# A linear-attention and channel-mix kernel: the arithmetic of the start moved between engines, and a new written order

## The chip, the cores and the metric

The kernel runs on one core of a Trainium2 chip. The metric is the device time of one execution in microseconds (us). A core has five engines that run side by side and meet through semaphores: TensorE (PE; its weight loads are PEld), VectorE (DVE), ScalarE (ACT), GpSimd (POOL) and SyncE (SP). Transfers between device memory (HBM) and on-chip memory (SBUF) are issued by SP, ACT or POOL and moved by 16 transfer engines (DMA).

## The reference

The input is q, k, v of shape (8 batches, 8 heads, 576 positions, 64), then the weights of a channel mix. The attention part is linear: a softmax of q over the head dimension, a softmax of k over the positions, and two small products. The channel mix shifts the sequence by one position, mixes it with two vectors mu, and runs three products.

```python
q_s = exp(q - max(q, -1));  q_s /= sum(q_s, -1)
k_s = exp(k - max(k, 2));   k_s /= sum(k_s, 2)
kv  = einsum('bhsd,bhse->bhde', k_s, v)
x   = einsum('bhsd,bhde->bhse', q_s, kv)        # as (B, S, 512)
x_prev = x shifted by one position
xk = mu_k * x + (1 - mu_k) * x_prev
xr = mu_r * x + (1 - mu_r) * x_prev
k  = maximum(xk @ w_k, 0)                       # 512 -> 1024
v  = k * k @ w_v                                # 1024 -> 512
r  = sigmoid(xr @ w_r)                          # 512 -> 512
out = r * v                                     # float32
```

The kernel leaves out the subtraction of the maxima, which cancels, and writes the sigmoid as a tanh.

## The kernel before, in words

The work of a batch b is split into two halves of its heads, g = 0 and 1, and in batches 0 and 1 each load and exponential is split once more (n = 0, 1). The names in the written order are built from these digits: `expq001` is the exponential of q for batch 0, half 0, part 1. For one (b, g):

- `load…q/k/v`: the transfers into a ring of eleven raw buffers `raw_a` to `raw_k` (L201), and `load0gv` into `vb` (L216). Batches 1 to 7 are loaded through GpSimd's queue, batch 0's q and k through the queues of SyncE and ScalarE. Eight semaphores serve GpSimd's transfers in turn, so a transfer is not issued before the one eight places earlier has landed.
- `expq`, `expk` (ScalarE, L325), `cast` (ScalarE, L331: v to bf16), `rsum`, `rrec`, `scale` (VectorE, L340, L344, L349: the softmax of q).
- `T`, `KV`, `Z` (TensorE): transpose of q, k times v, and the sums of k; for later batches one block `TKV` or `B`. `rz` and `kvn` or `w` (VectorE) normalise, `qt` (ScalarE) copies the transpose out.
- In batches 0 and 1 the mixing with mu is folded into the small weights: `wp…0` for xk and `wp…1` for xr (L466, two instructions each) multiply the normalised kv by mu and by 1 - mu; `X…0`, `X…1` (L478) are the products, and `x…` copies them into `xk` and `xr`, the first part on ScalarE and the second on VectorE (L488, L491). These need `wide` (a matmul that spreads mu over all partitions), `widecopy` (ScalarE, L279) and `rest` (L275: 1 - mu).
- Later batches use `xb`, `xs`, `edge`, `diff`, `sc`, `mix` instead, with mu as a column (`muload`, `mu`, `mucopy`).

The channel mix runs over units of up to 512 positions. In unit i, `ki0` to `ki7` (TensorE, L600) are the eight column blocks of x @ w_k, each four matmuls; in units 0 and 1 the first four are cut into two halves (`k01`, `k01.2`), the first needing only g = 0. `relu` (ScalarE, L587) and `sq` (VectorE, L591) follow. `r` (L632) and `v` (L652) are the other products, `th` (ScalarE, L637) the tanh, `o` (VectorE, L658) the gated output, `st` the store. The weights come through GpSimd's queue too: `wk00` to `wk11` (tiles `wk_aa`, `wk_ab`, `wk_ba`, `wk_bb`), `wr`, and `wv0` to `wv2` (`wv_a` to `wv_c`).

Nothing is scheduled at run time. `ORDER` is a string of some 950 names that fixes the order on every engine and in every queue; the digits behind a colon are the buffer that the step takes (`k01:2` takes PSUM bank 2, `mm_c`), `ACT!load…` puts a load in ScalarE's queue, and `fill.4^expq001` makes a step wait for another. An engine works through its names strictly in this order, so a step that waits for a transfer holds all that stands behind it on its engine. `fill` (L291) is a matmul of zeros that nobody reads; before the change seventeen of them stand among the first steps, held by steps of the softmax.

## Time and profile before

| | |
|---|---|
| time, median of 3 | 200.34 us (200.0 to 200.4) |
| the profiled execution's own time | 199.95 us |
| its span, first to last instruction | 198.2 us |
| TensorE busy | 186.0 us, 94% of the span |
| VectorE, ScalarE, GpSimd busy | 150.7, 146.3, 45.8 us |
| moved by the transfer engines | 40.13 MB, mean 202 GB/s |

A row of the order in time gives the start in us, the duration in us, the engine, the line of the kernel, the operation, its output and inputs with their shapes, and in brackets how long the engine was idle before it and what ended that. Rows of several like instructions are merged (x8). A row of the busy time by stage gives the stage, its length, then the busy time of each engine with the number of instructions, the granted TensorE clock, the busy share of the transfer engines (above 1 where packets of several queues overlap), and the GB/s that they moved. Buffer letters are part of the names (`mm_a` is PSUM bank 0, `raw_k` the eleventh raw buffer).

### The profile page before, as it was taken

The numbers are of one execution on the slowest core, as the hardware profiler recorded it, in microseconds if no ns is written. First come the engines' busy times: TensorE is split into PE (matmuls) and PEld (weight loads), VectorE is DVE, ScalarE is ACT, GpSimd is POOL, SyncE is SP. The second block draws the span as 40 slices with busy tenths as digits, with TensorE's granted clock in tenths as the row PEclk, the third lists the DMA queues.
The fourth block names the chain that finished last, engine by engine and source line by source line (L and its number), as shares of the span: only waits on it lengthen the run. The fifth ranks groups of instructions, "written<-read, shape, count | busy, mean of one in ns | idle before, by whom it ended". The sixth has DMA issues, their size and how long they took to land.

```text
span 198.2 us, 5164 instructions
## 1 busy us (share of the span) xinstructions
PE 186.0 (94%) x2060; PEld 93.2 (47%) x2084; DVE 150.7 (76%) x342; ACT 146.3 (74%) x225; POOL 45.8 (23%) x75
## 2 busy tenths in 40 slices
PE   1898999999999999999999999999999999999992
PEld 0374445434544544445565545554444544444751
DVE  0797468999989999999999995999825459732531
ACT  2678898799999999999999497877624762662340
POOL 7449357954324302712000000000000000000000
PEclk9999999999999999999999999999999999999999
DMA  6999999999999997899932230422044013402513
GB/s 200 310 289 288 273 341 202 393 394 398 416 390 390 401 412 281 291 392 406 369 98 55 59 77 3 106 56 53 3 108 108 0 29 80 106 2 56 122 37 106
DMA packets 16544, 40.13 MB, mean 202 GB/s; under 512 B 2300, under 2 KB 5640, under 8 KB 16520
## 3 DMA queue, kind: packets, MB, share of 16 engines
q0 software_dynamic: 9440, 27.99, 42.5%
q1 hardware_dynamic: 6120, 10.07, 18.5%
q10 hardware_dynamic: 960, 1.74, 2.6%
q8 instruction: 16, 0.26, 0.5%
q14 instruction: 8, 0.07, 0.1%
HBM read 33.56 MB, written 9.44 MB: 217 GB/s over the span
## 4 chain that ended last, share of the span: by engine, by line
PE 51%; issue 1%; ACT 0%; DVE 0%
PE mm_b L652 7%; PE mm_a L652 6%; PE mm_a L600 5%; PE mm_b L600 4%; PE mm_d L652 4%; PE mm_c L600 4%; PE mm_d L600 4%; PE mm_c L632 3%; PE mm_c L652 3%; PE mm_d L632 3%; PE mm_a L632 2%; PE mm_b L632 1%; PE att_b L516 1%; PE att_a L516 1%; PE att_a L390 1%
## 5 line engine op out<-in xcount | busy, mean ns | idle before, releaser
L652 PEld LDWEIGHTS <-k_a 128*128 128x128 bf16 x144 | 13.7, 98 | 16.9 <-DVE k_a L591 0.6
L632 PEld LDWEIGHTS <-xr 128*128 128x128 bf16 x144 | 13.9, 98 | 16.4 <-issue 0.2
L652 PEld LDWEIGHTS <-k_b 128*128 128x128 bf16 x152 | 14.3, 98 | 15.1 <-issue 0.6
L632 PE MATMUL mm_c<-wr,xr 128*128 128x512 bf16 x48 | 13.0, 379 | 0.2
L600 PEld LDWEIGHTS <-wk_bb 128*128 128x128 bf16 x80 | 7.8, 98 | 7.7
L600 PEld LDWEIGHTS <-wk_ab 128*128 128x128 bf16 x80 | 7.7, 98 | 8.1 <-DVE xk L488 0.6
L600 PEld LDWEIGHTS <-wk_ba 128*128 128x128 bf16 x80 | 7.7, 98 | 7.8 <-issue 0.5
L600 PEld LDWEIGHTS <-wk_aa 128*128 128x128 bf16 x80 | 7.4, 98 | 8.3 <-issue 0.9
L632 PE MATMUL mm_d<-wr,xr 128*128 128x512 bf16 x35 | 9.2, 379 | 0.1
L591 DVE TENSOR_TENSOR k_a<-rel_b 128x512 bf16<-128x512 bf16 (+1 forms) x13 | 5.3, 405 | 5.2 <-ACT rel_b L587 5.2
L587 ACT ACTIVATE rel_c<-mm_c 128x512 bf16<-128x512 f32 (+1 forms) x8 | 4.5, 568 | 4.0 <-PE mm_c L600 4.0
L587 ACT ACTIVATE rel_a<-mm_c 128x512 bf16<-128x512 f32 (+1 forms) x7 | 4.1, 582 | 4.3 <-PE mm_c L600 4.3
L632 PE MATMUL mm_a<-wr,xr 128*128 128x512 bf16 x28 | 7.2, 379 | 0.1
L632 PE MATMUL mm_b<-wr,xr 128*128 128x512 bf16 x28 | 7.2, 379 | 0.0
L591 DVE TENSOR_TENSOR k_b<-rel_c 128x512 bf16<-128x512 bf16 (+1 forms) x13 | 5.2, 401 | 2.3 <-ACT rel_c L587 2.0
L291 PE MATMUL mm_c<-still 128*128 128x256 bf16 x8 | 3.3, 412 | 3.9 <-ACT eq_a L325 3.9
L587 ACT ACTIVATE rel_a<-mm_b 128x512 bf16<-128x512 f32 (+1 forms) x10 | 6.0, 598 | 1.2 <-PE mm_b L600 1.2
L591 DVE TENSOR_TENSOR k_b<-rel_a 128x512 bf16<-128x512 bf16 (+1 forms) x14 | 5.4, 388 | 1.8 <-ACT rel_a L587 1.4
L600 PE MATMUL mm_b<-xk,wk_ab 128*128 128x512 bf16 (+1 forms) x22 | 6.1, 360 | 0.3 <-DVE xk L488 0.3
L591 DVE TENSOR_TENSOR k_a<-rel_a 128x512 bf16<-128x512 bf16 (+1 forms) x14 | 5.6, 399 | 1.1 <-ACT rel_a L587 1.0
L587 ACT ACTIVATE rel_b<-mm_c 128x512 bf16<-128x512 f32 (+1 forms) x6 | 3.2, 537 | 4.3 <-PE mm_c L600 4.3
L591 DVE TENSOR_TENSOR k_b<-rel_b 128x512 bf16<-128x512 bf16 (+1 forms) x13 | 5.0, 387 | 1.7 <-ACT rel_b L587 1.3
(361 smaller groups left out, 562.5 us busy)
## 6 DMA issues: line engine op xcount, KB each, us to landing
out_dram<-th_a SPq DMA_DIRECT2D x13, 128.0 KB, 5.7
out_dram<-th_b SPq DMA_DIRECT2D x12, 128.0 KB, 3.4
...
raw_k<-in_v_dram POOLq DMA_DIRECT2D x2, 576.0 KB, 7.1
raw_b<-in_q_dram POOLq DMA_DIRECT2D x2, 576.0 KB, 10.0
raw_e<-in_q_dram POOLq DMA_DIRECT2D x2, 576.0 KB, 10.8
```

What stands on the lines that cost most here:

```text
L291: return kn.nc.tensor.matmul(kn.bank(slot)[:, 0:256], lhsT=kn.still[:, 0:128], rhs=kn.still[:], start=True, stop=True)
L390: kn.nc.tensor.matmul(kn.half(slot, r)[two[u], KVO:KVO + n], lhsT=kn.eks[ek.index][two[r], j, u, :], rhs=by, start=(j == 0), stop=(j == J ...
L516: kn.nc.tensor.matmul(kn.half(slot, u)[two[r], to:to + n], lhsT=kn.ws[w.index][two[u], r, :], rhs=kn.qts[qt.index][two[u], r, 64 + at:64 + ...
L587: kn.nc.scalar.activation(out=kn.rels[rel.index][:, 0:n], in_=kn.bank(kf)[:, 0:n], func=ACT.Relu, scale=HALF_ROOT)
L591: kn.nc.vector.tensor_tensor(out=kn.k2s[k2.index][:, fc, 0:n], in0=kn.rels[rel.index][:, 0:n], in1=kn.rels[rel.index][:, 0:n], op=ALU.mult)
L600: kn.nc.tensor.matmul(kn.bank(kf)[:, 0:n], lhsT=kn.wk[fc // 4][ct % 2][:, ct // 2, (fc % 4) * 128: (fc % 4) * 128 + 128], rhs=kn.xs[0][:, ...
L632: kn.nc.tensor.matmul(kn.bank(rps), lhsT=kn.xs[1][:, ct, c:c + 128], rhs=kn.wr[:, ct, :], start=(ct == 0), stop=(ct == CT - 1))
L652: kn.nc.tensor.matmul(kn.bank(vps)[:, 0:width], lhsT=kn.k2s[k2.index][:, ft, 128 * m:128 * m + 128], rhs=wv_of(ft)[:, part], start=(ft == ...
```

## The change

- `rest` (1 - mu) runs on VectorE instead of GpSimd.
- The r weights of batch 0 (`wp001`, `wp011`) run on VectorE; GpSimd computes those of batch 1 (`wp101`, `wp111`) only.
- The zero matmuls are 24 instead of 17: twenty of them stand in one run ahead of `wide`, the first waiting for the exponential table's first use (`warm`), and four more before `T00` and `KV001`.
- A newly searched order: from the start to about unit 2 the steps and the loads stand in another sequence; from `o11` of unit 1 on the sequence of names is, but for one load, the same, and only bank and buffer numbers differ.

```diff
@@ -32,7 +32,7 @@
-FILLS = 80
+FILLS = 24
...
-ACT!load00q1:0 zero load00v load01q1:1 ACT!load00k0:2 load00q0 ident ACT!load01q0 rows
-ACT!load00k1 load01k1:3 load01v consts warm load10q1:4 load10v0:5 ACT!load01k0 wk10 expq001:0
-fill:3 fill.2:2 wk00 fill.3:3 rsum001:0 fill.4^expq001:2 expq000 fill.5:3 fill.6:2 wk01 rrec001
-fill.7:3 expq011:1 fill.8^rsum001:2 scale001:0 fill.9^expq000:3 load11q0:6 fill.10:2 expk000:0
-fill.11:3 rsum000 fill.12^scale001:2 fill.13:3 fill.14^expk000:2 rsum011:1 wide:0 expq010 rrec011
-rrec000 scale000 rsum010 T00:0 fill.15:3 scale011:1 expk001 fill.16:2 fill.17:3 rrec010 widecopy
-KV001:1 scale010 expk011:1 KV000 rest late Z00 expk010 KV011:3 rz00:0 load10k1:7 qt00:0 KV010
-kvn00:0 T01:2 wp000:0 wp001 Z01 qt01:1 edge00 rz01:1 X000:1.0 kvn01:1 wk11 wp010:1 X001:3.2 x0000
-load10q0 x0001 x0010 edge01 wr x0011 X010:1.0 k01:2 load11v0:8 x0100 x0101 k02:3 expq101:2 wp011
-k03:0 cast100:0 k00:1 load11q1 k02.2 expq110:0 k00.2 wv0 relu02:0 k03.2 k01.2 load11v1 X011:0.1
-relu01:1 load10v1 k05:3 relu03:2 sq01:0 load10k0 rsum101:2 relu00:1 k07:2 load11k0:9 expq100 sq02
-x0111 x0110 k04:0 sq00 relu07:0 k06:1 relu04:1 load11k1 cast110:1 r00:2 sq04 muload wv1 rsum110:3
-relu06:1 r03:0 wv2 sq03 th00:0 expq111 r01:1 relu05:2 rsum111 r02:2 th03:1 rsum100 th01:2
-load20v0:10 v010:3 expk101:2 rrec100 rrec101 sq07 th02:3 rrec111 v030:0 rrec110 sq05 cast111
-scale100:2 cast101 v000:1 load20q0:0 scale101 expk100 v020:2 load21q0:1 scale110:0 expk110:0
-load20k0:2 scale111 expk111 TKV10:1 TKV11:0 rz10:2 kvn10:0 qt10:2 wp101:0 v021 rz11:0 kvn11:1 v011
-sq06 load21v0:3 qt11:0 wp100 v031 v001 edge10 load30q0:4 v012 edge11 load30v0:6 cast200:2 v022 o01
-X100:1.0 load21k0:8 wp110:1 v002 x1000 x1001 load31q0:5 v032 o00 mu:3 wp111 X110:1.0 o02 k13:1
-x1100 load40q0:7 x1101 k11:2 expq200:1 expq210:2 rsum200:0 load31k0:9 k13.2 k11.2 load30k0:10
-relu13:0 X111:1.0 mucopy o03 expk200:1 k12:3 x1111 st03 k14:1 load40v0:0 x1110 rrec200 st00.2
-rsum210:1 relu11:2 k10:0 st00 X101:0.1 relu14:1 st01 load31v0:1 cast210:0 sq11:1 st03.2 k10.2 sq13
-st02.2 k12.2 x1011 relu10:2 k15:2 x1010 sq10 k16:1 scale200:1 load41q0:2 relu12:0 relu15:2 k17:0
-expq300:0 rrec210 sq14 r10:3 sq12 relu17:1 rsum300:2 TKV20:1 relu16:0 cast300:1 load40k0:3 r11:2
-rrec300 rz20:1 scale210:2 th10:4 r13:0 expk210:2 r12:1 w20:0 sq16 qt20:1 scale300:0 v100:3
-load50q0:4 th11:5 B21:0.1 sq15 expq310:1 sq17 v120:2 rz21:2 load41k0:6 w21:1 th13:6 rsum310:3
...
+ACT!load00q0:0 zero ident load00q1 ACT!load00k0:1 load01q1:2 ACT!load01q0 rows load00v consts warm
+load00k1 load10q1:3 late load01k0:4 load01v wk01 expq000:0 expq001 wk00 expk000:0 rsum001:0 wk10
+ACT!load01k1 rsum000 expq011:1 load10q0 rrec001 scale001:0 wk11 rrec000 rsum011:1 fill^warm:1
+fill.2:2 fill.3:3 fill.4:0 fill.5:1 fill.6:2 fill.7:3 fill.8:0 fill.9:1 fill.10:2 fill.11:3
+fill.12:0 fill.13:1 fill.14:2 fill.15:3 fill.16:0 fill.17:1 fill.18:2 fill.19:3 fill.20:0 wide:0
+scale000 expq010 rrec011 rsum010 fill.21:1 fill.22:2 T00:0 load10v0:5 rrec010 scale011:1 widecopy
+expk001 scale010 qt00:0 fill.23:3 fill.24:1 KV001:1 rest KV000 T01:2 load11q0:6 expk010:1 Z00
+rz00:0 expk011 edge00 kvn00:0 KV010:0 expq101:2 wp000:0 load11q1 KV011 wp001 qt01:1 Z01 X000:3.1
+rz01:1 kvn01:1 load11v0:7 x0000 x0001 X001:0.2 wp010:1 x0010 k01:2 wr edge01 x0011 k02:3 X010:1.0
+wv0 k03:0 x0100 x0101 k00:1 load10k1:8 wp011 k01.2 k00.2 relu01:0 k03.2 load10k0 expq100 k02.2
+sq01:0 load11v1 rsum101:2 relu03:1 k05:2 cast100:0 load10v1 X011:0.1 relu02:2 load11k1:9 k04:0
+x0110 x0111 load11k0 relu00:0 sq02 k07:3 rsum100 cast110:1 sq00 relu05:2 k06:1 sq03 relu07:0 sq05
+r03:2 expq110:0 rrec100 wv1 relu06:1 rsum110:3 r02:3 relu04:2 expq111 r00:1 sq04 scale100:2 th02:0
+r01:0 th03:1 muload sq06 rrec110 th00:2 rrec101 rsum111 v000:3 th01:3 wv2 rrec111 expk101:2 v030:2
+scale111:0 expk100 load20v0:10 scale110 v020:1 cast111 load20q0:0 scale101 cast101 v010:0
+load21q0:2 expk111:0 load20k0:1 TKV10:0 expk110 load21v0:4 TKV11:1 rz10:2 kvn10:0 load30v0:3
+qt10:2 wp100:0 v011 rz11:0 v001 kvn11:1 sq07 v021 qt11:0 wp111:1 edge10 wp110 v012 v031 load30q0:6
+o01 X100:0.1 cast200:2 load21k0:8 v002 x1001 load31q0:7 x1000 v022 edge11 mu:0 expq200:1
+load31k0:5 o02 X110:1.0 mucopy v032 x1101 x1100 k11:1 load40q0:9 rsum200:0 expq210:0 k13:0
+X111:0.1 wp101 expk200:1 o00 k13.2 load30k0:10 k11.2 x1111 relu13:2 k14:3 o03 x1110 load31v0:0
+rrec200 k12:0 st03 rsum210:1 relu11:1 k10:2 st00.2 relu14:0 X101:1.0 st00 load41k0:2 cast210:0
+sq11:1 k10.2 st01 sq13 k12.2 x1011 st03.2 relu10:1 k15:1 st02.2 x1010 load40v0:1 sq10 scale200:1
+k16:3 relu12:2 relu15:1 k17:2 expq300:2 rrec210 sq14 sq12 r10:0 relu17:0 rsum300:3 relu16:2
+TKV20:0 load40k0:4 cast300:1 r11:1 rrec300 rz20:1 scale210:2 th10:4 r13:2 expk210:2 w20:0 r12:3
+sq16 qt20:1 scale300:0 load50q0:6 v100:0 th11:5 B21:1.0 sq15 expq310:1 sq17 v120:1 rz21:2 th13:6
...
@@ -224,7 +225,7 @@
                 tensor=src.tensor, offset=src.offset, ap=[[256, 2], [1, 256]]))
 
     def emit_warm():
-        kn.nc.scalar.activation(out=kn.warm[:], in_=kn.warm[:], func=ACT.Exp)
+        return kn.nc.scalar.activation(out=kn.warm[:], in_=kn.warm[:], func=ACT.Exp)
 
     def emit_first():
         nc = kn.nc
@@ -272,13 +273,13 @@
                                identity=kn.identf[:])
 
     def emit_rest():
-        kn.nc.gpsimd.tensor_scalar(out=kn.mu_wide[:, 1, :], in0=kn.mu_wide[:, 0, :],
+        kn.nc.vector.tensor_scalar(out=kn.mu_wide[:, 1, :], in0=kn.mu_wide[:, 0, :],
                                    scalar1=-1.0, scalar2=1.0, op0=ALU.mult, op1=ALU.add)
 
     wide_mm = add("PE", emit_wide, [rows_load, consts], [wide_slot], name="wide")
     wide_a = add("ACT", lambda: kn.nc.scalar.copy(out=kn.mu_wide[:, 0, :], in_=kn.bank(wide_slot)),
                  [wide_mm], [], [wide_slot], name="widecopy")
-    wide_done = add("POOL", emit_rest, [wide_a], name="rest")
+    wide_done = add("DVE", emit_rest, [wide_a], name="rest")
     mu_load = add("POOL", emit_mu_load, name="muload")
     mu_mm = add("PE", emit_mu, [mu_load, late_consts], [mu_slot], name="mu")
     mu_done = add("DVE", lambda: kn.nc.vector.tensor_copy(
@@ -463,7 +464,7 @@
 
             def mixed_weights(m):
                 for i in range(2):
-                    (kn.nc.gpsimd if m else kn.nc.vector).tensor_tensor(
+                    (kn.nc.gpsimd if m and b else kn.nc.vector).tensor_tensor(
                         out=kn.wps[wp.index][:, m, i, :],
                         in0=kn.kvns[kvn.index][:].rearrange("p a e -> p (a e)"),
                         in1=kn.mu_wide[:, i, 256 * m + 128 * g:256 * m + 128 * g + 128],
@@ -492,7 +493,7 @@
                              in_=kn.half(slots[t], u)[:, 0:288])
 
             for m in range(2):
-                wdone = add("POOL" if m else "DVE", lambda m=m: mixed_weights(m), [ndone, wide_done], [wp], [kvn], name=f"wp{tag}{m}")
+                wdone = add("POOL" if m and b else "DVE", lambda m=m: mixed_weights(m), [ndone, wide_done], [wp], [kvn], name=f"wp{tag}{m}")
                 slots = [Slot("any" if b == 0 else "att") for _ in range(2)]
                 o = add("PE", lambda m=m, slots=slots: mixed_x(m, slots),
                         [qdone, wdone], slots, [wp, qt], name=f"X{tag}{m}")

```

More of the change, by code (lines that the diff above doesn't have):

```diff
@@ new lines @@
+k85:0 sq83 relu84:1 k86:3 sq84 relu85:0 k87:2 sq85 relu86:2 r80:1 sq86 relu87:1 r81:0 sq87 th80:4
+v800:3 th81:1 v810:2 v801 v811 o80 r82:1 st80 o81 st80.2 r83:0 th82:0 st81 st81.2 v820:3 th83:6
+v830:2 v821 v831 o82 k90:1 st82 o83 k91:0 st82.2 relu90:0 k92:3 st83 relu91:2 sq90:1 k93:2
+relu92:1 sq91 st83.2 k94:1 relu93:0 sq92 k95:0 relu94:2 sq93 k96:3 relu95:1 sq94 k97:2 relu96:0
+sq95 r90:1 relu97:2 sq96 sq97 r91:0 th90:2 v900:3 th91:3 v901 v910:2 o90 v911 st90.2 st90 v910.2:1
+o91 v911.2 st91.2 st91 o91.2 st91.4 st91.3
```

89 lines of the change are left out of this document (42 added, 47 removed).

## The prediction

> **What bounds the kernel now.** I read the page first, then the busy time by stage, then the order in time of TensorE, ScalarE and GpSimd's queue, then the landings of transfers.
>
> ```profile
> span 198.2 us, 5164 instructions
> PE 186.0 (94%) x2060; PEld 93.2 (47%) x2084; DVE 150.7 (76%) x342; ACT 146.3 (74%) x225; POOL 45.8 (23%) x75
> DMA  6999999999999997899932230422044013402513
> ```
>
> ```profile
> core 0: us, PE busy (x) PEld busy (x) DVE busy (x) ACT busy (x) POOL busy (x), PEclk, DMA share, GB/s
> 12.00:30.00 18.00, 17.25 (x242) 9.54 (x241) 12.25 (x39) 15.52 (x28) 11.35 (x21) 1.00 1.15 295
> 30.00:35.00 5.00, 4.95 (x124) 2.79 (x124) 4.09 (x10) 4.04 (x8) 3.93 (x8) 1.00 1.03 205
> 45.00:95.00 50.00, 49.17 (x628) 23.69 (x635) 48.38 (x99) 49.41 (x70) 16.61 (x23) 1.00 0.99 379
> ```
>
> TensorE is busy 94% of the span, and in 45 to 95 it is busy 49.17 of 50 us, so a microsecond won or lost before 45 should reach the end nearly whole. But the transfer engines are full (a 9 in the DMA line, a share of about 1 in the stages) from the second slice to about 95 us. The next question is which of the two decides when TensorE may go on in the first 48 us.
>
> ```profile
> 14.73 0.54 PE L478 MATMUL att_b<-qt_a,wp_a 64*64 64x288 bf16 x8
> ...
> 17.77 0.39 PE L600 MATMUL mm_c<-xk,wk_aa 128*128 128x512 bf16 x1
> ...
> 19.50 0.59 PE L600 MATMUL mm_d<-xk,wk_ab 128*128 128x512 bf16 x2
> ...
> 25.40 0.81 PE L632 MATMUL mm_c<-wr,xr 128*128 128x512 bf16 x3
> ...
> 36.65 0.44 PE L478 MATMUL att_b<-qt_c,wp_a 64*64 64x288 bf16 x8
> ...
> 38.39 0.44 PE L478 MATMUL att_b<-qt_a,wp_b 64*64 64x288 bf16 x8
> ...
> 39.01 0.61 PE L600 MATMUL mm_b<-xk,wk_aa 128*128 128x512 bf16 x2
> ...
> 42.09 0.59 PE L600 MATMUL mm_d<-xk,wk_aa 128*128 128x512 bf16 x2 [0.17 <-DVE mu L284]
> ...
> 47.99 0.38 PE L632 MATMUL mm_d<-wr,xr 128*128 128x512 bf16 x1
> ```
>
> ```profile
> 36.44 1.15 ACT L331 CAST vv_c<-raw_k 128x1152 bf16<-128x1152 f32 x1 [0.33 <-DMA raw_k<-in_v_dram]
> 37.50 0.63 ACT L488 CAST xk<-att_b 128x576 bf16<-128x576 f32 x1
> 38.88 0.64 ACT L488 CAST xk<-att_b 128x576 bf16<-128x576 f32 x1 [0.75 <-PE att_b L478]
> 39.41 1.17 ACT L325 ACTIVATE eq_b<-raw_a 128x1152 bf16<-128x1152 f32 x1
> 40.60 1.16 ACT L325 ACTIVATE eq_c<-raw_b 128x1152 bf16<-128x1152 f32 x1
> ...
> 42.15 1.15 ACT L325 ACTIVATE ek_b<-raw_c 128x1152 bf16<-128x1152 f32 x1
> ```
>
> ```profile
> 11.43 0.61 POOL L275 TENSOR_SCALAR mu_wide<-mu_wide 128x512 f32<-128x512 f32 x1 [4.20 <-ACT mu_wide L279]
> ...
> 15.90 0.76 POOL L299 DMA_DIRECT2D wr<-in_moe_w_r_dram  x1
> ...
> 28.60 0.74 POOL L299 DMA_DIRECT2D wv_b<-in_moe_w_v_dram  x1 [1.94 <-DMA wv_a<-in_moe_w_v_dram]
> ...
> 30.08 0.73 POOL L201 DMA_DIRECT2D raw_k<-in_v_dram  x1
> 30.82 0.73 POOL L201 DMA_DIRECT2D raw_a<-in_q_dram  x1
> 31.54 0.72 POOL L201 DMA_DIRECT2D raw_b<-in_q_dram  x1
> 32.27 0.72 POOL L201 DMA_DIRECT2D raw_c<-in_k_dram  x1
> ```
>
> ```profile
> wr<-in_moe_w_r_dram POOLq DMA_DIRECT2D x1, 512.0 KB, 8.7
> ```
>
> ```profile
> raw_k<-in_v_dram POOLq DMA_DIRECT2D x1, 576.0 KB, 6.3
> raw_a<-in_q_dram POOLq DMA_DIRECT2D x1, 576.0 KB, 8.4
> raw_b<-in_q_dram POOLq DMA_DIRECT2D x1, 576.0 KB, 9.0
> raw_c<-in_k_dram POOLq DMA_DIRECT2D x1, 576.0 KB, 9.8
> ```
>
> The last two fences give time from issue to landing, so issue plus that time is the landing. wr lands at 15.90 + 8.7 = 24.60, and its first reader (the r product, L632) starts at 25.40: a margin of 0.8. Batch 2's four loads land at 36.38 (raw_k), 39.22 (raw_a), 40.54 (raw_b) and 42.07 (raw_c); their readers on ScalarE start at 36.44 (after an idle 0.33), 39.41, 40.60 and 42.15, that is 0.06 to 0.19 behind. Up to 42 us the kernel already runs at the heels of its transfers.
>
> **The change part by part.** *The start.* The zero matmuls now wait for the exponential table (L227) and run 20 in a row, then wide. They and wide only have to be over when ScalarE wants widecopy, some 2 us before VectorE wants `rest`, so they cost nothing; if they ran late they would hold widecopy and every ScalarE instruction behind it. What sets X000 (14.73) is VectorE's chain of sums and scalings.
>
> ```profile
> 5.83 0.75 DVE L340 TENSOR_REDUCE rsum_a<-eq_a 128x9 f32<-128x576 bf16 x1 [2.91 <-ACT eq_a L325]
> ...
> 9.31 0.76 DVE L349 TENSOR_TENSOR qs_a<-eq_a,rrec_a 128x576 bf16<-128x576 bf16 x1
> ...
> 11.56 1.09 DVE L349 TENSOR_TENSOR qs_b<-eq_b,rrec_b 128x576 bf16<-128x576 bf16 x1
> ...
> 13.76 1.04 DVE L466 TENSOR_TENSOR wp_a<-kvn_a,mu_wide 128x128 bf16<-128x128 f32 x2
> ```
>
> The chain still begins with rsum001, behind two exponentials on ScalarE, so at about 5.8. Its last scaling takes 1.09 beside GpSimd's L275 and 0.76 without it (row at 9.31): 0.33 won. The constants of `late`, now ahead of the chain, give some 0.3 more. `rest` moves to VectorE: L275's 0.61 is the nearest price, 1.09 (the dearest row above) the upper bound, and a faster engine could make it nearly nothing. It stands between the last scaling and rz00, and rz00 waits for T01 and Z00 on TensorE anyway, which cover about a microsecond; without that cover X000 would be its 0.61 later, still ahead of before. Batch 0's r weights add at most 1.04 for two instructions, behind the k weights, so X000 does not wait for them. X000 starts at about 14.73 - 0.33 - 0.3 = 14.1.
>
> *The first k products.* After X000 the new order has k01 and k02 ahead of X010, and the copies x0000 and x0001 first on their engines. X000 plus one X step (38.39 to 39.01: 0.62) plus a copy (0.63 at 37.50) and a wait for VectorE's kvn of 0.2 gives k01 at about 15.6 instead of 17.77. Then k01, k02, X010, its copies and k03, k00 (four halves took 17.77 to 19.50, 0.43 each): the second halves start near 17.9 instead of 19.50. So 1.6 us are won here. This is what the change could give, 200.34 - 1.6 = 198.7, if nothing came late behind it.
>
> *GpSimd's queue.* L275 and batch 0's four L466 leave it, and the loads are reordered: v, q10, v, three wk, q10, the fourth wk, v10, q11 twice, v11, then wr, wv_a, and the rest of batch 1. Before wr there now stand four weights and eight other loads where seven stood: one more load of 288 KB. Freeing the queue moves issues, but the transfer engines were full: from 12 to 30 us share 1.15. At the 295 GB/s of that stage 288 KB take 1.0 us (0.75 at 379), so wr lands at 24.6 + 0.75 to 1.0 = 25.35 to 25.6. The k products and X011 end at 25.40 - 1.6 = 23.8, some 24.3 with a wait for the fourth wk. TensorE then stands idle for 1.1 us: r starts at about 25.4, as before, and the 1.6 us are gone. What is late next is wr.
>
> *Batch 2's loads.* The same bytes stand ahead of them as before. wv_b moves ahead of the mu loads, so its issue no longer stands behind the idle 1.94 us at 28.60, and part of the thin stage 30 to 35 (205 GB/s) is filled: 5 us at 205 GB/s are 1.03 MB, which the 295 of the stage before would move in 3.5 us, so at most 1.5 us are to be had; the least is nothing. The stage also carries the converting weight loads, and the first v load now starts behind ident, some 0.6 us later (three instructions that GpSimd runs first), which gives some back; with a share of 1.03 I take a landing 0.3 us earlier, near the lower end.
>
> *ScalarE's order from 36 us.* Before: cast200, x1000, x1100, expq200, expq210, relu13, expk200. Now: cast200, x1000, **expq200**, x1100, expq210, **expk200**, relu13. Two instructions that TensorE needs, x1100 and relu13, stand behind loads. With landings 0.3 earlier: expq200 at 38.95, x1100 one step later (36.44 to 37.50: 1.06) at 40.0 to 40.65. X111's second half waits for x1100 and ends at 41.0; k13.2, k11.2, k14 (four pairs, 0.43 each) end at 42.7. expk200 cannot start before 41.8 and is through by 42.85, relu13 by 43.45. k12 takes the bank that relu13 empties, so TensorE idles 0.8 us and starts k12 at 43.5. Before, k12 to r10 took 42.09 to 47.99 = 5.90 with k14 (0.86) between: 5.04 remain. r10 starts at 43.5 + 5.04 = 48.55 instead of 47.99: **0.56 later**. From there the two orders are the same but for bank numbers, and TensorE has no slack to win it back.
>
> The sum against the profiled execution: 199.95 + 0.56 = 200.5. That execution lies 0.39 under the median of three, 200.34, so I forecast 200.34 + 0.56 = **200.9**.
>
> *The clock.* The granted clock reads 1.00 in every stage, but the zero matmuls show half speed:
>
> ```profile
> 1.28 0.42 PE L291 MATMUL mm_c<-still 128*128 128x256 bf16 x1
> 1.49 0.42 PE L291 MATMUL mm_d<-still 128*128 128x256 bf16 x1
> ```
>
> 0.21 us for 256 columns is 0.82 ns a column; a half of a k product, two matmuls of 512, takes 0.43, or 0.42 ns a column. So the array runs at half speed at the start and at full speed by the k products. The Trainium skill (TensorE: Matmul & The Clock Gate, Part 1: The HAM clock gate) says that the array runs at half clock until a free-running window of about 3.4 us was busy, and again after an idle one. By that rule the new dense run, about 4.2 us, wakes the clock early, and the sparse stretch from 9 to 13 us may put it to sleep again before X000; what half speed there would cost is the last rival below.
>
> **The rivals.** *Faster: the loads were held by their issue, not by bandwidth.* If the queue without L275 and L466 keeps the engines so supplied that the thin stage goes, batch 2 lands 1.5 us earlier. Then no load is waited for: after x1000 (ending at 38.1) expq200, x1100, expq210, expk200 and relu13 run back to back on ScalarE and relu13 ends at 42.4 (three steps of 1.06, two copies); k12 starts there and r10 at 47.45, 0.55 earlier: 199.8. If wr, too, lands 0.5 us earlier, the time is 199.3. For it speak the idle 1.94 at 28.60 and the 205 GB/s; against it the share of 1.03 in the same stage. It decides from a landing 0.85 us earlier, where r10 is level with before.
>
> *No change.* Landings 0.5 to 1.0 earlier put r10 within 0.4 us of before: 200.3.
>
> *The array back at half speed at X000.* Between the dense run and X000 TensorE has little to do. If X000 and the first k products (14.1 to 17.9, 3.8 us) ran at half speed for most of that time, up to 1.7 us would be added; the idle before wr takes 1.1 of it, so r would start 0.6 late, and the time would be 200.9 + 0.6 = 201.5. Against it: transposes and products of batch 0 still stand in that stretch, as they do in the trace of before.
>
> **How the numbers follow.** Forecast (slower, 200.9): 0.41. Faster by the loads: 0.26. No change: 0.27. Clock: 0.06. A measurement of this kernel tells about 0.2%, 0.4 us, from no change. So slower 0.47, same 0.27, faster 0.26. The low end, 199.3, is the first rival with wr early too; the high end is the half-speed case, 201.6. The forecast's own range is 200.75 to 201.3 (landings unmoved: +0.85).
>
> **What would show it.** k01 near 15.6 and the second halves near 18; a TensorE wait of about 1 us ahead of L632 put down to wr; the first L632 at 25.2 to 25.7; expq200 and expk200 starting on their landings at 38.9 and 41.8; a TensorE wait ahead of k12 put down to ScalarE's L587. Wrong would be: batch 2's loads landing more than 0.85 us earlier, L632 starting under 24.7 with those loads early too, or no wait at k12.

## The result, and the profile after

The changed kernel takes 199.58 us (median of 21 runs, 199.03 to 200.40); the kernel before, in runs taken beside it, 200.43 us (21 runs, 199.76 to 201.15). The ratio is 0.9955, 95% interval 0.9942 to 0.9967: some 0.85 us **faster**, where I had forecast 200.9. The profiled execution took 199.41 us with a span of 197.6 (before: 199.95 and 198.2). Line numbers of the changed kernel are one higher than before.

The page of the changed kernel, its head and its line of transfers:

```profile
span 197.6 us, 5180 instructions
...
PE 187.6 (95%) x2067; PEld 94.6 (48%) x2091; DVE 150.8 (76%) x345; ACT 146.0 (74%) x225; POOL 43.5 (22%) x70
...
DMA  6999999999999996999932320422044013403413
```

The busy time by stage (columns as in the prediction: the last three are granted clock, transfer share and GB/s):

```profile
12.00:30.00 18.00, 17.72 (x242) 9.62 (x239) 12.57 (x37) 14.89 (x29) 8.11 (x14) 1.00 1.16 293
30.00:35.00 5.00, 4.95 (x124) 2.83 (x124) 3.47 (x10) 4.29 (x8) 4.39 (x7) 1.00 1.14 282
...
45.00:95.00 50.00, 49.39 (x629) 23.71 (x636) 48.34 (x97) 49.43 (x70) 16.24 (x23) 1.00 1.00 378
```

One stage has changed: from 30 to 35 us the transfers move 282 GB/s instead of 205, at a share of 1.14 instead of 1.03. That is 77 GB/s for 5 us, or 0.39 MB more, which at the 378 GB/s of the last row takes 1.0 us (an estimate).

TensorE in order of time:

```profile
14.74 0.45 PE L479 MATMUL mm_c<-qt_a,wp_a 64*64 64x288 bf16 x1
...
16.87 0.59 PE L601 MATMUL mm_c<-xk,wk_aa 128*128 128x512 bf16 x2
...
19.54 0.59 PE L601 MATMUL mm_c<-xk,wk_ab 128*128 128x512 bf16 x2
...
25.44 0.81 PE L633 MATMUL mm_c<-wr,xr 128*128 128x512 bf16 x3
...
37.99 0.44 PE L479 MATMUL att_b<-qt_a,wp_b 64*64 64x288 bf16 x8
...
42.81 0.59 PE L601 MATMUL mm_a<-xk,wk_aa 128*128 128x512 bf16 x2 [0.28 <-ACT rel_c L588]
...
47.85 1.03 PE L633 MATMUL mm_a<-wr,xr 128*128 128x512 bf16 x4
```

X000 starts where it did (14.74, before 14.73), the r products too (25.44 and 25.40). r10 is only 0.14 earlier than before. ScalarE from batch 2's loads on:

```profile
37.64 1.16 ACT L326 ACTIVATE eq_b<-raw_a 128x1152 bf16<-128x1152 f32 x1
38.71 0.62 ACT L489 CAST xk<-att_b 128x576 bf16<-128x576 f32 x1
39.67 1.16 ACT L326 ACTIVATE eq_a<-raw_c 128x1152 bf16<-128x1152 f32 x1 [0.34 <-DMA raw_c<-in_q_dram]
41.11 1.16 ACT L326 ACTIVATE ek_b<-raw_b 128x1152 bf16<-128x1152 f32 x1 [0.28 <-DMA raw_b<-in_k_dram]
42.18 0.58 ACT L588 ACTIVATE rel_c<-mm_a 128x512 bf16<-128x512 f32 x1
42.66 0.63 ACT L489 CAST xr<-att_a 128x576 bf16<-128x576 f32 x1
```

GpSimd's queue, and the time from issue to landing:

```profile
15.78 0.75 POOL L300 DMA_DIRECT2D wr<-in_moe_w_r_dram  x1 [0.73 <-DMA wk_aa<-in_moe_w_k_dram]
...
25.37 0.71 POOL L300 DMA_DIRECT2D wv_b<-in_moe_w_v_dram  x1 [1.86 <-DMA wr<-in_moe_w_r_dram]
27.92 0.53 POOL L268 DMA_DIRECT2D mu_sb<-in_moe_mu_k_dram  x1 [1.84 <-DMA wv_a<-in_moe_w_v_dram]
...
30.23 0.75 POOL L202 DMA_DIRECT2D raw_k<-in_v_dram  x1
31.23 0.73 POOL L202 DMA_DIRECT2D raw_a<-in_q_dram  x1 [0.25 <-ACT ek_c L326]
31.95 0.72 POOL L202 DMA_DIRECT2D raw_c<-in_q_dram  x1
32.67 0.72 POOL L202 DMA_DIRECT2D raw_b<-in_k_dram  x1
```

```profile
raw_k<-in_v_dram POOLq DMA_DIRECT2D x1, 576.0 KB, 5.8
raw_a<-in_q_dram POOLq DMA_DIRECT2D x1, 576.0 KB, 6.4
raw_c<-in_q_dram POOLq DMA_DIRECT2D x1, 576.0 KB, 7.6
raw_b<-in_k_dram POOLq DMA_DIRECT2D x1, 576.0 KB, 8.4
```

Batch 2's loads are issued 0.15 to 0.41 us later than before, but land sooner: at 36.03, 37.63, 39.55 and 41.07, against 36.38, 39.22, 40.54 and 42.07. The last three are 1.0 to 1.6 us earlier. wv_b, issued 3.2 us earlier than before, itself lands at 33.17 and so no earlier (before: 28.60 + 4.5 = 33.10). What has changed is how much of the work ahead of batch 2's loads was done by then.

Where did 0.14 us at r10 become 0.5 at the end? Three rows of before and two of after answer it (ScalarE's x1110 of before; TensorE at B21 and its last group, before and after):

```profile
43.20 0.63 ACT L488 CAST xr<-att_b 128x576 bf16<-128x576 f32 x1
53.54 0.22 PE L516 MATMUL att_a<-qt_b,w_a 64*64 64x64 bf16 x4 [0.19 <-ACT qt_b L368]
193.90 0.38 PE L652 MATMUL mm_c<-wv_c,k_b 128*128 128x256 bf16 x2
```

```profile
53.14 0.22 PE L517 MATMUL att_b<-qt_b,w_a 64*64 64x64 bf16 x4
193.38 0.38 PE L653 MATMUL mm_b<-wv_c,k_b 128*128 128x256 bf16 x2
```

Before, TensorE at 53.54 waits for ScalarE. After, ScalarE's x1110 starts 0.54 earlier (42.66 against 43.20), that wait is gone, B21 starts 0.40 earlier and the last group 0.52. So the pace behind 43 us is ScalarE's as much as TensorE's, and x1110 is the mark to follow. The table of all kernels gives it: the start of ScalarE's x1110, the start of TensorE's last group and their distance, each from the one profiled execution, beside the median and its ratio to runs of the kernel before on the same chip.

| kernel | median | ratio (95%) | x1110 | last group | distance |
|---|---|---|---|---|---|
| before | 200.43 | | 43.20 | 193.90 | 150.70 |
| changed | 199.58 | 0.9955 (0.9942-0.9967) | 42.66 | 193.38 | 150.72 |
| e1 wv_b behind mu | 200.47 | 1.0000 (0.9983-1.0018) | 43.66 | 194.36 | 150.70 |
| e2 mu on SyncE | 198.88 | 0.9922 (0.9895-0.9948) | 42.08 | 192.80 | 150.72 |
| e3 old, wv_b ahead | 200.36 | 0.9995 (0.9974-1.0015) | 44.30 | 195.00 | 150.70 |
| e4 GpSimd again | 199.62 | 0.9954 (0.9936-0.9973) | 42.65 | 193.33 | 150.68 |
| e5 more fills | 199.29 | 0.9935 (0.9923-0.9948) | 42.36 | 193.03 | 150.67 |
| e6 old ScalarE order | 199.69 | 0.9965 (0.9952-0.9977) | 42.81 | 193.55 | 150.74 |
| e7 ScalarE probe | 199.91 | 0.9980 (0.9968-0.9991) | 42.74 | 194.16 | 151.42 |
| e8 TensorE probe | 199.96 | 0.9973 (0.9964-0.9983) | 43.27 | 194.36 | 151.09 |
| e9 old, wv_b and ScalarE | 200.42 | 0.9997 (0.9980-1.0013) | 43.72 | 194.80 | 151.08 |
| e10 old, ScalarE order | 201.13 | 1.0035 (1.0023-1.0048) | 43.47 | 194.55 | 151.08 |
| e11 no dense run | 199.49 | 0.9956 (0.9939-0.9972) | 42.44 | 193.14 | 150.70 |
| e12 SyncE and fills | 198.85 | 0.9922 (0.9903-0.9941) | 42.08 | 192.78 | 150.70 |
| e13 old start | 199.78 | 0.9974 (0.9958-0.9990) | 42.95 | 193.65 | 150.70 |
| e14 new start | 200.23 | 0.9992 (0.9975-1.0010) | 44.20 | 194.93 | 150.73 |
| e15 old, three orders | 200.23 | 0.9995 (0.9980-1.0011) | 43.13 | 194.22 | 151.09 |
| e16 old, mu on SyncE | 201.27 | 1.0059 (1.0037-1.0080) | 44.41 | 195.12 | 150.71 |

The distance is 150.67 to 150.74 in thirteen of the eighteen. Single executions of one kernel lie up to 1.8 us apart (e3: 199.41 to 201.20), so a row's x1110 belongs to that execution and not to the median: the execution shown of before is 0.48 under its median, that of e3 0.71 over (201.07), that of e14 0.76 over (200.99).

### The profile page after: what moved, and what is told of

Read it like the earlier page. It is cut to its first block, busy times and chain, and to the rows that moved or that the text cites. A ratio compares the mean times of both kernels' runs of the same rounds, so it can differ in the third digit from the quotient of the medians.

```text
span 197.6 us, 5180 instructions
## 1 busy us (share of the span) xinstructions
PE 187.6 (95%) x2067; PEld 94.6 (48%) x2091; DVE 150.8 (76%) x345; ACT 146.0 (74%) x225; POOL 43.5 (22%) x70
## 3 DMA queue, kind: packets, MB, share of 16 engines
q1 hardware_dynamic: 6264, 10.36, 19.1%
## 4 chain that ended last, share of the span: by engine, by line
PE 51%; issue 1%; ACT 0%; DVE 0%
PE mm_d L653 7%; PE mm_c L653 6%; PE mm_c L601 5%; PE mm_d L601 4%; PE mm_a L653 4%; PE mm_b L601 4%; PE mm_a L601 4%; PE mm_b L633 3%; PE mm_b L653 3%; PE mm_a L633 3%; PE mm_c L633 2%; PE mm_d L633 1%; PE att_a L517 1%; PE att_b L517 1%; PE att_b L391 1%
## 5 line engine op out<-in xcount | busy, mean ns | idle before, releaser
L633 PEld LDWEIGHTS <-xr 128*128 128x128 bf16 x144 | 13.9, 98 | 16.4 <-issue 0.2
L633 PE MATMUL mm_b<-wr,xr 128*128 128x512 bf16 x45 | 12.2, 379 | 0.2
L633 PE MATMUL mm_a<-wr,xr 128*128 128x512 bf16 x39 | 10.2, 379 | 0.1
L588 ACT ACTIVATE rel_b<-mm_b 128x512 bf16<-128x512 f32 (+1 forms) x9 | 5.1, 571 | 4.0 <-PE mm_b L601 4.0
L633 PE MATMUL mm_c<-wr,xr 128*128 128x512 bf16 x28 | 7.2, 379 | 0.0
L592 DVE TENSOR_TENSOR k_a<-rel_c 128x512 bf16<-128x512 bf16 (+1 forms) x15 | 6.0, 402 | 1.3 <-ACT rel_c L588 1.2
L588 ACT ACTIVATE rel_c<-mm_d 128x512 bf16<-128x512 f32 (+1 forms) x10 | 6.0, 602 | 1.2 <-PE mm_d L601 1.2
L588 ACT ACTIVATE rel_c<-mm_b 128x512 bf16<-128x512 f32 (+1 forms) x6 | 3.5, 580 | 4.3 <-PE mm_b L601 4.3
L292 PE MATMUL mm_b<-still 128*128 128x256 bf16 x7 | 2.9, 413 | 3.7 <-ACT warm L228 3.7
L601 PE MATMUL mm_d<-xk,wk_ba 128*128 128x512 bf16 (+1 forms) x22 | 6.1, 359 | 0.1
L292 PEld LDWEIGHTS <-still 128*128 128x128 bf16 x24 | 3.1, 140 | 6.4 <-ACT warm L228 3.7
```

The source lines that it names most:

```text
L292: return kn.nc.tensor.matmul(kn.bank(slot)[:, 0:256], lhsT=kn.still[:, 0:128], rhs=kn.still[:], start=True, stop=True)
L588: kn.nc.scalar.activation(out=kn.rels[rel.index][:, 0:n], in_=kn.bank(kf)[:, 0:n], func=ACT.Relu, scale=HALF_ROOT)
L592: kn.nc.vector.tensor_tensor(out=kn.k2s[k2.index][:, fc, 0:n], in0=kn.rels[rel.index][:, 0:n], in1=kn.rels[rel.index][:, 0:n], op=ALU.mult)
L601: kn.nc.tensor.matmul(kn.bank(kf)[:, 0:n], lhsT=kn.wk[fc // 4][ct % 2][:, ct // 2, (fc % 4) * 128: (fc % 4) * 128 + 128], rhs=kn.xs[0][:, ...
L633: kn.nc.tensor.matmul(kn.bank(rps), lhsT=kn.xs[1][:, ct, c:c + 128], rhs=kn.wr[:, ct, :], start=(ct == 0), stop=(ct == CT - 1))
```

## The experiments

**Which part of the change brings the landing forward?** Four kernels: the moved weight load undone (e1), alone in the old kernel (e3), the moved instructions put back on GpSimd (e4), and the mu loads taken off GpSimd's queue altogether (e2).

e1, the changed kernel:

```
-r03:2 expq110:0 rrec100 wv1 relu06:1 ... th03:1 muload sq06
+r03:2 expq110:0 rrec100 relu06:1 ... th03:1 muload wv1 sq06
```

> Theory 1 (the order of the loads: wv_b issued ahead of the two small mu loads keeps the transfer engines busy between 30 and 35 us): with wv_b behind the mu loads again it is issued at about 28.6 instead of 25.4, spots under a share of 1 come back near 30 to 35, raw_b (batch 2's k) lands at about 42.0 instead of 41.07, and as ScalarE has relu13 behind that load now, x1110 comes near 43.6 instead of 42.66: the time is 0.5 to 1.0 us above the changed kernel, 200.1 to 200.6. Theory 2 (GpSimd freed of the 1 - mu instruction and of batch 0's r weights made the loads early): landings stay at 41.1 and the time at 199.6. Theory 3 (the start of the kernel gave the gain): 199.6 too.

Measured 200.47: the whole gain is gone. ScalarE's row on batch 2's k is exactly 1.0 later than in the changed kernel, x1110 at 43.66, and two spots under a share of 1 are back (stages of e1):

```profile
42.11 1.17 ACT L326 ACTIVATE ek_b<-raw_b 128x1152 bf16<-128x1152 f32 x1 [0.28 <-DMA raw_b<-in_k_dram]
```

```profile
30.00:31.00 1.00, 1.00 (x7) 0.41 (x6) 0.97 (x3) 1.00 (x3) 0.97 (x2) 1.00 0.85 149
...
34.00:35.00 1.00, 0.95 (x40) 0.63 (x40) 0.93 (x5) 0.70 (x1) 0.93 (x2) 1.00 0.88 322
```

Batch 2's k lands at 42.07, as before the change. Theory 1 holds, and 2 and 3 fall, for the changed kernel: without wv_b ahead of the mu loads nothing is gained.

e4, the changed kernel:

```
-    wide_done = add("DVE", emit_rest, [wide_a], name="rest")
+    wide_done = add("POOL", emit_rest, [wide_a], name="rest")
-                    (kn.nc.gpsimd if m and b else kn.nc.vector).tensor_tensor(
+                    (kn.nc.gpsimd if m else kn.nc.vector).tensor_tensor(
```

(and the two engine names that go with them).

> The changed kernel with 1 - mu and batch 0's r weights back on GpSimd, orders as changed. Theory 1: GpSimd waits for landings most of the time in 10 to 30 us anyway, so the loads go at the same times within 0.3 us, raw_b lands at 41.0 to 41.3, and the time is 199.5 to 199.9 even if X000 comes up to 0.5 later. Theory 2: the loads behind those instructions go 0.6 to 0.9 later each, raw_b lands near 42, and the time is back at 200.4.

Measured 199.62, x1110 at 42.65: moving those five instructions to VectorE is worth nothing here, as theory 1 has it.

e2, the changed kernel:

```
-load00k1 load10q1:3 late load01k0:4 load01v ... th03:1 muload sq06
+load00k1 load10q1:3 late load01k0:4 muload load01v ... th03:1 sq06
-            kn.nc.gpsimd.dma_start(out=kn.mu_sb[4 * m:4 * m + 4, :], in_=bass.AP(
+            kn.nc.sync.dma_start(out=kn.mu_sb[4 * m:4 * m + 4, :], in_=bass.AP(
```

(and the engine name that goes with it).

> The changed kernel with the two small mu loads on SyncE's queue, behind the first loads, instead of GpSimd's. Theory A (GpSimd's queue lets a load go only when the eighth load before it has landed, and the two small loads use up two of the eight places): wv_c and raw_k (batch 2's v) are issued some 1.5 us earlier, raw_b lands some 0.5 us earlier, at 40.6, ScalarE's idle 0.28 ahead of it goes, and the time is 199.1 to 199.3. Theory B (the transfer engines are full from 26 to 45 us, share 1.0 and more in every microsecond, so an earlier issue only waits longer): landing and time unchanged, 199.4 to 199.8.

Measured 198.88, better than theory A hoped. Its queue and its ScalarE row:

```profile
28.38 0.73 POOL L202 DMA_DIRECT2D raw_k<-in_v_dram  x1
```

```profile
40.54 1.16 ACT L326 ACTIVATE ek_b<-raw_b 128x1152 bf16<-128x1152 f32 x1 [0.27 <-DMA raw_b<-in_k_dram]
```

raw_k goes out 1.85 earlier, raw_b is there 0.57 earlier, x1110 is 0.58 and the median 0.70 earlier. This fits the waits in the changed kernel's queue above: wv_b, the eighth transfer issued behind wr (wv_a and six half loads of batch 1 lie between), goes out when wr has landed (25.08), and the first mu load, the eighth behind wv_a, when wv_a has. These are the eight places that the description of the kernel names, and two loads of 2 KB hold two of them. Theory B, that the engines were full anyway, was wrong: from 26 to 45 us the changed kernel's share lies between 0.94 and 1.30 in every microsecond, and an earlier issue was still worth something. From 25 to 36 us e2 moves 349 GB/s at a share of 1.11, the changed kernel 332 at 1.10.

e3, the kernel before:

```
-cast110:1 r00:2 sq04 muload wv1 rsum110:3
+cast110:1 r00:2 sq04 wv1 muload rsum110:3
```

> The kernel before, with wv_b's load moved ahead of the two mu loads and nothing else. Theory 1: wv_b issued at about 25.4, batch 2's loads land about 1.0 us earlier (raw_c, its k, at 41.1 instead of 42.07), expk200 starts behind it and ScalarE and all that follows come 0.5 to 1.0 earlier: 199.5 to 199.9, all of the measured gain by one moved load. Theory 2 (GpSimd's freed instructions) and theory 3 (the start): unchanged, 200.4.

Measured 200.36: no gain, against my theory. In its trace raw_a is issued at 30.88 and lands 6.5 later, at 37.4, and batch 2's k lands at 41.52 (before: 42.07), but ScalarE does not use it:

```profile
40.11 0.64 ACT L488 CAST xk<-att_b 128x576 bf16<-128x576 f32 x1 [1.10 <-PE att_b L478]
40.65 1.17 ACT L325 ACTIVATE eq_b<-raw_a 128x1152 bf16<-128x1152 f32 x1
```

In the old order x1100, which waits for TensorE's X110, stands ahead of expq200. That execution also started late (r at 26.64, before 25.40), so the wait of 1.10 is longer than the 0.75 of before; but before, too, expq200 stands at 39.41 behind x1100, and an earlier landing does not move it. In the changed kernel the moved load is necessary (e1); in the old one it is not sufficient.

**Does the start count?** e5 keeps the array warm; e11 leaves the dense run out.

e5, the changed kernel:

```
-FILLS = 24
+FILLS = 32
-fill.21:1 fill.22:2 T00:0 ... KV000 T01:2
+fill.21:1 fill.22:2 fill.25:3 fill.26:1 fill.27:2 T00:0 ... KV000 fill.28:1 fill.29:3 fill.30:1 fill.31:3 T01:2
```

> The changed kernel with seven more zero matmuls, three ahead of T00 and four ahead of T01 (up to 1.5 us of matmul time at half speed, put where TensorE waits for VectorE), so that the array does not fall back to half speed ahead of X000. Theory 1 (the landing of batch 2's loads decides): X000 runs at full speed and k01 starts near 15.6 instead of 16.9, but raw_b (batch 2's k) lands at 41.0 to 41.2 as before, and the time is 199.4 to 199.8. Theory 3 (the start decides): the 0.7 to 1.2 us gained at k01 reach the end, 198.4 to 198.9.

```profile
14.48 0.41 PE L479 MATMUL att_b<-qt_a,wp_a 64*64 64x288 bf16 x8
...
16.84 0.39 PE L601 MATMUL mm_c<-xk,wk_aa 128*128 128x512 bf16 x1 [1.27 <-DMA wk_aa<-in_moe_w_k_dram]
```

X000 runs at full speed now, 0.41 for eight matmuls instead of 0.69, and TensorE is free for k01 at 15.57, within 0.05 of the 15.6 that I had predicted. There it waits 1.27 us for wk_aa, which lands at 16.77, so k01 and the r products (25.43) come no earlier than in the changed kernel. In the changed kernel's execution wk_aa did not hold k01: wr's issue, which waits for wk_aa, goes out at 15.78 there. In nine kernels with this start it lands at 15.2 to 15.9, in the two with the added fills at 16.8 (e5) and 16.4 (e12); why it is later there no run shows. The time is 199.29; its interval (0.9923 to 0.9948) overlaps the changed kernel's (0.9942 to 0.9967), so whether the fills bring 0.3 us or nothing stays open.

e11, the changed kernel:

```
-rrec000 rsum011:1 fill^warm:1 fill.2:2 ... fill.20:0 wide:0
+rrec000 rsum011:1 wide:0
```

> The changed kernel without the dense run: its first 20 zero matmuls are left out, the four later ones stay. Theory (the transfers decide, and the array is at half speed at X000 with the dense run too): X000 within 0.2 of 14.4, raw_b lands near 41.1, 199.4 to 199.8. Rival (the run keeps the clock up): the array reaches full speed later, k01 and the r products come 0.5 or more later, and where that delays x1100, the time is 200.0 or more.

Measured 199.49, X000 at 14.15, x1110 at 42.44: the dense run of twenty zero matmuls is worth nothing.

e12 has the edits of e2 and e5 together. Expected were x1110 near 42.1 and 198.8 to 199.0 if the landing decides, 198.5 to 198.6 if the start adds its part. It gave 42.08 and 198.85, against 198.88 in e2: beside the earlier loads, the fills bring nothing that can be told from zero.

**What carries the gain to the end?** e6 undoes ScalarE's order; e7 and e8 delay one engine each.

e6, the changed kernel:

```
-mu:0 expq200:1 load31k0:5 ... x1101 x1100 k11:1 ... wp101 expk200:1 o00 ... relu13:2 k14:3
+mu:0 load31k0:5 ... x1101 x1100 expq200:1 k11:1 ... wp101 o00 ... relu13:2 expk200:1 k14:3
```

> The changed kernel with ScalarE's old order around batch 2's loads: x1100 ahead of expq200, relu13 ahead of expk200. Theory S (from 43 us on ScalarE's unbroken stream sets the pace): x1100 now waits for X110, which ends at 38.7, expq200 starts at 39.2, expq210 at 40.3, relu13 at 41.4, expk200 at 41.85, x1110 at 42.9 instead of 42.66, and the time is 0.2 to 0.3 later, 199.8 to 199.9. Theory P (TensorE sets the pace and k12's wait for relu13 is what counts, as the prediction's step has it): relu13 is done by 41.9, TensorE's idle 0.28 ahead of k12 goes, and the time is 0.3 to 0.56 earlier, 199.0 to 199.3.

x1110 comes at 42.81 (42.9 expected by S), the time is 199.69, so 0.1 later, which the intervals do not tell from nothing; the 0.3 to 0.56 us earlier of theory P, my prediction's step, are out. The new order of ScalarE is no loss in this kernel.

e7 and e8, the changed kernel, one added step each (the code of the two probes is left out):

```
-o03 x1110 load31v0:0
+o03 x1110 probe load31v0:0
-cast300:1 r11:1
+cast300:1 probe:1 r11:1
```

> The changed kernel with two added copies of 128x256 zeros on ScalarE behind x1110 (about 0.25 us each, 0.5 in all) that nothing reads. Theory S: everything behind comes 0.5 later, 200.1. Theory P: ScalarE has slack there, 199.6 to 199.7.

> The changed kernel with four added zero matmuls of 256 columns on TensorE ahead of r11 at about 49 us (0.11 us each, 0.43 in all). Theory S: TensorE runs ahead of ScalarE and takes the 0.43 out of later waits, 199.6 to 199.75. Theory P: all of it reaches the end, 200.0. If both probes cost their full length, the two engines are level and the time follows whichever is delayed.

```profile
43.26 0.85 ACT L253 COPY spare<-still 128x256 bf16<-128x256 bf16 x2
```

```profile
50.20 0.61 PE L253 MATMUL mm_b<-still 128*128 128x256 bf16 x4
```

In the traces both cost nearly all they take. The copies hold ScalarE for 0.76 us (43.26 to 44.02, the next instruction), and the distance from x1110 to the end grows by 0.70 (151.42); the matmuls grow it by 0.37 of their 0.43. The medians say less for ScalarE: 0.33 us (0.5 by the ratios), and 0.38 for TensorE, where the intervals of e8 and the changed kernel overlap a little. So the two engines are nearly level behind 43 us: most of what either loses there is lost. (e8's own landing was 0.6 later in that execution, ahead of its probe, hence x1110 at 43.27.)

**What else does the old kernel need?** e9 and e10 are the kernel before with ScalarE's new order, with and without wv_b moved (e9 has e3's edit as well).

```
-mu:3 wp111 X110:1.0 o02 ... k11:2 expq200:1 expq210:2 ... relu13:0 X111:1.0 mucopy o03 expk200:1 k12:3
+mu:3 wp111 expq200:1 X110:1.0 o02 ... k11:2 expq210:2 ... expk200:1 relu13:0 X111:1.0 mucopy o03 k12:3
```

> The kernel before with two orders of the change and nothing else: wv_b's load ahead of the mu loads, and on ScalarE expq200 ahead of x1100 and expk200 ahead of relu13. The end of the last matmul has followed ScalarE's x1110 by 151.1 us in every run so far. Theory: the earlier load was useless alone because x1100, which waits for TensorE's X110 until 38.9, stood ahead of expq200; with both, expq200 starts at 37.5 to 38.4, expk200 at 41.1 to 41.6, x1110 at 42.7 to 43.1 (before: 43.20), and the time is 199.9 to 200.2. Rival (the start of the changed kernel is needed too): no gain, 200.4.

> The kernel before with ScalarE's new order alone. With the loads landing as before (39.2, 40.5, 42.07) expk200 stays at 42.1 and relu13 comes behind it: x1110 at 43.65 instead of 43.20 and TensorE's k12 some 0.5 later, so 0.3 to 0.5 slower, 200.7 to 200.9: the price that the prediction put on this order. Rival (the order costs nothing): 200.4.

e10 is 201.13, 0.70 above: the price that I had put on this order (0.56) is real, with the old landings and TensorE's old order. With wv_b moved (e9) it falls to 200.42, 0.71 less than e10, but no better than before and outside the 199.9 to 200.2 that I expected. By the medians the moved load is worth 0.71 with ScalarE's new order and 0.07 with the old one (e3). The traces do not show why: batch 2's k lands no earlier in e9's execution than in e10's (the first row is e9, which in this execution is 0.46 over its median).

```profile
42.17 1.16 ACT L325 ACTIVATE ek_b<-raw_c 128x1152 bf16<-128x1152 f32 x1 [0.34 <-DMA raw_c<-in_k_dram]
```

```profile
41.92 1.16 ACT L325 ACTIVATE ek_b<-raw_c 128x1152 bf16<-128x1152 f32 x1 [0.35 <-DMA raw_c<-in_k_dram]
```

The next two split the change in time. Each is one kernel's order up to the first r product and the other's from there:

```
 e13:  fill:3 ... r00:2 sq04 (order and code of before)   then  ... wv1 relu06 ... muload ... (order of the changed kernel)
 e14:  fill^warm:1 ... expq110 rrec100 (changed kernel)   then  ... muload wv1 ...            (order of before)
```

> The kernel before up to the first r product (its fills, its GpSimd instructions, its orders: all that is issued ahead of the mu loads and wv_b), and from there the order of the changed kernel on every engine and queue, buffers numbered anew. Theory A (the gain lies in the orders from 25 us on: wv_b ahead of the mu loads, two of the next loads ahead of GpSimd's weights for batch 1, one v part moved behind X100 and X110): raw_b or its counterpart lands near 41.1, x1110 comes near 42.7, 199.5 to 199.9. Theory B (the start is needed): 200.3 to 200.5.

> The reverse: the changed kernel up to the first r product (dense run, VectorE's 1 - mu and r weights, the new order of the first loads), and from there the order of the kernel before. Theory A: x1110 near 43.2 and 200.3 to 200.6, nothing of the gain left. Theory B: the gain stays, 199.5 to 199.9. If this and the reverse both come out near 200.0, each part brings some of it.

199.78 and 200.23: the old start with the new orders keeps 0.65 of the 0.85 us by the medians (0.5 of 0.9 by the ratios), the new start with the old orders nothing that can be told from zero. In the traces batch 2's k lands at 41.38 in e13 and at 41.98 in e14. This is theory A, and it rules out e9's rival. e14 also shows what the old order makes of a late start. Its instructions up to the r products are those of the changed kernel, but in this execution, the longest of its twelve, the array stayed at half speed longer, and r came 1.09 us later:

```profile
16.87 1.01 PE L599 MATMUL mm_c<-xk,wk_aa 128*128 128x512 bf16 x2
...
26.53 1.03 PE L631 MATMUL mm_c<-wr,xr 128*128 128x512 bf16 x4
```

x1100 then waits 1.10 for X110 and expq200 behind it, as in e3, and x1110 comes at 44.20.

e15 and e16 look for the rest: e9 with two more loads ahead of GpSimd's weights, and the old kernel with the mu loads on SyncE (the lines that change their engine are those of e2). The edits show what each adds to e9 and to the kernel before.

```
-load20k0:2 scale111 expk111 TKV10:1 ... wp101:0 ... sq06 load21v0:3 qt11:0 ... edge10 load30q0:4 v012
+load20k0:2 scale111 expk111 load21v0:3 load30q0:4 TKV10:1 ... wp101:0 ... sq06 qt11:0 ... edge10 v012
```

> The kernel before with wv_b ahead of the mu loads and ScalarE's new order (200.42 with these two), and now also the next two loads ahead of GpSimd's r weights for batch 1, which wait for kvn and held those loads until 36. Theory: with them in the queue the transfer engines have no spot under a share of 1 at 34 to 36, batch 2's k lands at 41.2 to 41.5, x1110 comes near 42.9 and the time is 199.7 to 200.0, as with the old start and all the new orders (199.78). Rival (those loads stand behind batch 2's in the queue and can't bring them earlier; it is TensorE's order that was missing): 200.3 to 200.5.

```
-load01k1:3 load01v consts ... sq04 muload wv1
+load01k1:3 muload load01v consts ... sq04 wv1
```

> The kernel before with the two mu loads on SyncE's queue and nothing else. The loads of batch 2 land 1.0 to 1.5 earlier. If ScalarE's x1100, which waits for X110 until 38.9 and stands ahead of expq200, holds the old order whatever the loads do: expq200 stays at 39.4, expk200 at 42.0, and the time is 200.2 to 200.4. If the landing alone decides: x1110 1.0 earlier, 199.4.

e15 is 200.23, between its theory and the rival, and not to be told from e9. Its trace has expk200 at 41.59 and x1110 at 43.13, near the expected 42.9, but TensorE loses what is left:

```profile
43.29 0.59 PE L600 MATMUL mm_b<-xk,wk_ba 128*128 128x512 bf16 x2 [0.68 <-ACT rel_a L587]
```

k14 waits for relu13, which stands behind expk200. All three old kernels with that order (e9, e10, e15) have a distance of 151.08 to 151.09, 0.38 more than the others; e13, with TensorE's new order (the last v part behind X110, k14 ahead of k12), has 150.70. So what the old kernel lacks is probably TensorE's order, with which it has enough to do until relu13. e6 points the same way: with ScalarE's old order but TensorE's new one it keeps nearly all of the gain (199.69), as X110 ends earlier there and x1100 starts at 38.49 instead of the 38.88 of before. This is argued from what is left over; the old kernel with wv_b moved and TensorE's order alone was not run.

e16 is slower by 0.84 and a bad test: with the two transfers added there, its start came late. ScalarE's own load, which went out at 4.74 before, goes out at 6.07 there, and the first exponential starts at 6.45 instead of 5.12. Its r products are 1.34 late (26.74), X110 with them, and x1110 is at 44.41. Its expectation is not tested by this; it shows only that the old order passes a late start on to the end.

## Why the prediction was wrong

I forecast slower with 0.47. The landing of batch 2 came 1.0 us earlier, which is the condition of my rival "No change" (0.27, landings 0.5 to 1.0 earlier), and r10 came where that rival puts it. The time came out near the rival "Faster" (0.26, 199.8), which wanted landings 1.5 us earlier and r10 at 47.45. So that 199.8 is close is partly luck: r10 was at 47.85, and the rest was won where I saw nothing. That rival's reason, a queue without L275 and L466, is worth nothing (e4). Step by step:

- **Batch 2's landing, the step that failed.** I took 0.3 us earlier, between 0 and 1.5, because the share of 1.03 read as full. Measured: 0.35 for v, but 1.6, 1.0 and 1.0 for the three loads that matter. Batch 2's own issues came 0.15 to 0.41 later, so it is not these that were held; the thin stage ahead of them filled (205 to 282 GB/s), and putting wv_b back empties it again and takes the gain (e1). I had both clues: the description of the kernel says that a transfer waits for the one eight places earlier, and a fence shows wv_b's idle 1.94 us for wv_a. I did not count the places in the new order. There wv_b waits for wr (25.08) and no longer for wv_a, and the two mu loads wait in its stead. How wv_b, which lands no earlier, lets the loads behind it land earlier the runs do not show in detail.
- **From r10 to the end, the second step that failed.** I took r10's shift as the shift of the end, "TensorE has no slack". Had the landing been right, my own sum would have given almost no change: with batch 2's k at 41.07 it puts r10 0.14 earlier, as the trace has it. The end moved 0.52, because ScalarE, 49.4 of 50 us busy from 45 to 95, was the later of the two before (the wait of 0.19 at 53.54) and gained 0.54 at x1110.
- **ScalarE's order.** The mechanism is real: relu13 behind expk200 makes TensorE idle ahead of k12. The size in this kernel was 0.28, not 0.8, with the landing 1.0 earlier. In the old kernel the order costs 0.70 (e10); here undoing it brings nothing (e6).
- **The start.** I put k01 at 15.6 and the second halves at 17.9; they came at 16.87 and 19.54, so the 1.6 us were never won. Two terms were missing, X000's own delay of 0.64 (next item) and its half speed. k01 starts behind VectorE's copy of X000's second part:

```profile
15.97 0.76 DVE L489 CAST xk<-att_b 128x576 bf16<-128x576 f32 x1 [0.53 <-PE att_b L479]
```

From X000 to that copy it is 1.23 us here and 0.74 in e5 (14.21 to 14.95), so half speed cost about 0.5 (an estimate from the two traces). wr landed at 25.08 (15.78 + 9.3), 0.5 later than before, but the k products were not done sooner, so TensorE did not wait for it. That r starts as before was right, for a wrong reason.

- **X000 at 14.1.** 14.74 in the profiled execution and 14.15 to 14.35 in e1, e2, e4 and e11, which share its start but for what they change: right within 0.25 there, and of no use. I had said that the dense run and wide cost nothing unless they ran late, and in the profiled execution they did. All twenty fills ran at half speed, and ScalarE's widecopy waited 1.52 us for wide; in e4, where the array woke during the run, it started at 8.87.

```profile
10.19 0.59 ACT L280 COPY mu_wide<-mm_a 128x512 f32<-128x512 f32 x1 [1.52 <-PE mm_a L262]
```

- **The clock.** My last rival, half speed at X000, happened: eight of its matmuls take 0.69 us where e5's take 0.41. e4, with the dense run in it, shows how:

```profile
8.77 0.28 PE L292 MATMUL mm_b<-still 128*128 128x256 bf16 x1
8.89 0.27 PE L292 MATMUL mm_c<-still 128*128 128x256 bf16 x1
...
14.83 0.69 PE L479 MATMUL att_b<-qt_a,wp_a 64*64 64x288 bf16 x8
```

The run had woken the array (two fills 0.12 apart, where half speed takes 0.21), and by X000 it was at half speed again. The price in the changed kernel's execution was that 0.5 us at k01, where I had put 0.6 at r; where the half speed lasted longer (e14), r came 1.09 later. The Trainium skill (TensorE: Matmul & The Clock Gate, Part 1: The HAM clock gate) says that the window watched, about 3.4 us, runs freely and that an idle one halves the clock. As to waking, the trace agrees: the same run of 4.3 us woke the array in e4 and did not in the changed kernel's profile, where all twenty fills are 0.21 apart. As to falling back, it does not: e4's granted clock goes to 0.50 at 10.7 us, 3.4 us after the fills had come to full speed at 7.3, though TensorE was busy for 2.82 us of the 3.40 between and never idle for longer than 0.58.

- **The range.** Two of its ends do not follow from the working: unmoved landings give 200.34 + 0.85 = 201.2, not 201.3, and the half-speed case was worked out as 201.5, not 201.6.
